# The order of four DMA transposes and two weight loads at the start of a GEGLU kernel

## The chip, the cores and the metric

One core of a Trainium2 chip. The metric is the device time of one execution in microseconds (us). The span, which the profile shows, leaves out what lies around the program: 1.7 to 2.9 us in the runs on record, so the time has a spread of its own that the span has not.

## The reference

```python
B, S, D, F = 1, 2048, 1024, 3584          # everything bf16
def reference(x, w_gate, w_up, w_down):
    return (gelu(x @ w_gate) * (x @ w_up)) @ w_down      # tanh form of GELU
```

## The kernel before

The products are made in halves of S and mostly by a Strassen scheme (the matmuls of L381 and L617). Only the first chunk of 512 columns of F, for the first half of S (1024 tokens), is done with plain products: these are the matmuls of L245, grouped in eight "units". A unit is 128 columns of F by one block of 512 tokens: 8 matmuls of gate and 8 of up, one for each 128-wide block of D. The first two units share their walk through D and are called `first_units`; the third is `unit(hT, PB, 2, 0)`.

x has to be transposed. For the first token block, D blocks 0 to 3 are loaded plainly and transposed by TensorE; D blocks 4 to 7 come by four DMA transposes ("transpose 4" to "transpose 7" below). The first chunk's weights are loaded in two halves of columns: columns 0 to 255 (`FA = 256`), for the first two units, and columns 256 to 511, for the third and fourth, called here the **gate half** (of `w_gate`) and the **up half** (of `w_up`), 512 KB each. SP (SyncE) issues these transfers; the texts below call its queue, or the part of it at one DMA engine, a ring. All that the change touches is the order in which SP issues them, and the order of the 32 matmuls of the first two units:

```python
    for j in range(2):                                   # j: 0 gate, 1 up
        load_w(first, j, KH, KD, sp, 0, FA)              # D blocks 4..7, columns 0..255
    for kd in range(KH, KD):
        load_xT(xT, 0, 0, kd, kd + 1)                    # transposes 4, 5, 6, 7
    for j in range(2):
        load_w(first, j, 0, KD, sp, FA, FG)              # gate half, up half
    for k0 in range(0, KD, KH):
        load_xT(xT, 0, 1, k0, k0 + KH)                   # second token block, 4 D blocks each
    # ... (cut)
    def first_units(hT):
        wg, wu = chunks[first]
        held = (VB, RB)
        transpose_x0(0)
        for q in range(NXQ):                             # pairs of D blocks
            for kd in (2 * q, 2 * q + 1):
                for u in range(2):
                    mm_gu(banks[held[u][0]], wg, u, 0, kd)
            for kd in (2 * q, 2 * q + 1):
                for u in range(2):
                    mm_gu(banks[held[u][1]], wu, u, 0, kd)
                # ... (cut)
```

## Time and profile before

| | before |
|---|---|
| time, median of 6 | 543.49 us (543.32 to 544.40) |
| span of the profiled run | 541.7 us |
| TensorE busy | 533.9 us, 99% |
| first Strassen matmul in the chain that ended last | 34.83 us |
| from there to the start of the last instruction | 503.51 us |

### The profile page before, as it was taken

The page shows a single profiled execution, that of the slowest core. Times are in us where ns is not written, and L with a number is a line of the kernel's source. Part 1 is how long each engine was busy: PE and PEld are TensorE (multiplying, and loading weights), DVE is VectorE, ACT ScalarE, POOL GpSimd, SP SyncE. Part 2 cuts the span into 40 slices and gives each one's busy share as a digit, 9 for nine tenths or more (in the row PEclk, how much of TensorE's full clock was granted, in tenths as well). Part 3 has the DMA queues.
Part 4 walks back from the last instruction along what each step waited for, and adds up shares of the span by engine and source line. Part 5 has one row for each costly group of instructions (what it writes and reads, how often), then busy time and mean ns, then how long its engine had stood idle before and what let it go on. Part 6 is the DMA issues. An engine that isn't in the chain of part 4 may idle for free.

```text
span 541.7 us, 7194 instructions
## 1 busy us (share of the span) xinstructions
PE 533.9 (99%) x2356; PEld 372.6 (69%) x2392; DVE 350.5 (65%) x465; ACT 258.4 (48%) x433; POOL 239.5 (44%) x206
## 2 busy tenths in 40 slices
PE   8999999999999999999999999999999999999997
PEld 3456777777677676767777766777767776866865
DVE  1646666887765899889574444444454469979961
ACT  2345555455555319216455555555555552462270
POOL 0097777888877000000057776677777630000000
PEclk9999999999999999999999999999999999999999
DMA  8956598898836979689952240404040457767946
GB/s 206 299 193 146 166 280 241 171 295 176 265 129 218 347 256 343 215 267 299 324 196 87 70 136 20 156 1 156 0 155 1 157 162 247 252 224 241 290 145 205
DMA packets 85924, 104.80 MB, mean 193 GB/s; under 512 B 18816, under 2 KB 67456, under 8 KB 85888
## 3 DMA queue, kind: packets, MB, share of 16 engines
q1 hardware_dynamic: 84816, 103.83, 61.5%
q10 hardware_dynamic: 1072, 0.52, 0.4%
q8 instruction: 19, 0.31, 0.3%
q14 instruction: 17, 0.14, 0.1%
HBM read 87.03 MB, written 13.63 MB: 186 GB/s over the span
## 4 chain that ended last, share of the span: by engine, by line
PE 96%; DMA 1%; SPq 1%; issue 0%; ACT 0%; ACTq 0%
PE bank L381 60%; PE bank L617 32%; PE bank L245 4%; DMA w_mem<-in_w_gate_dram 1%; SPq L172 1%; ACT o_sb L665 0%; ACTq L665 0%
## 5 line engine op out<-in xcount | busy, mean ns | idle before, releaser
L381 PE MATMUL bank<-t_mem,s_mem 128*128 128x512 f32 x1016 | 249.2, 399 | 0.0
L381 PEld LDWEIGHTS bank<-t_mem,s_mem 128*128 128x128 f32 x1016 | 190.9, 188 | 44.1
L355 POOL TENSOR_TENSOR s_mem<-w_mem 128x512 fp32r<-128x512 bf16 x100 | 117.4, 1194 | 197.7 <-DVE t_mem L238 103.3
L617 PE MATMUL bank<-t_mem,s_mem 128*128 128x512 f32 x560 | 130.2, 392 | 0.0
L404 DVE TENSOR_TENSOR bank<-bank,m 128x512 f32<-128x512 f32 x104 | 72.2, 698 | 83.0 <-ACT bank L424 74.3
L617 PEld LDWEIGHTS bank<-t_mem,s_mem 128*128 128x128 f32 x560 | 105.1, 188 | 22.9 <-issue 0.2
L269 DVE TENSOR_TENSOR hT<-w_mem,bank 128x512 bf16<-128x512 f32 x104 | 71.3, 687 | 59.9 <-ACT w_mem L264 24.8
L264 ACT ACTIVATE w_mem<-bank 128x512 f32<-128x512 f32 x104 | 61.8, 596 | 79.9 <-DVE bank L404 47.3
L381 PE MATMUL bank<-xT,w_mem 128*128 128x512 bf16 x391 | 97.5, 380 | 1.3
L381 PEld LDWEIGHTS <-w_mem 128*128 128x128 bf16 x416 | 36.6, 98 | 50.4 <-issue 13.1
L530 DVE TENSOR_TENSOR t_mem<-w_mem 128x1024 fp32r<-128x1024 bf16 x56 | 65.6, 1218 | 0.0
L355 POOL TENSOR_TENSOR s_mem<-w_mem,s_mem 128x512 fp32r<-128x512 bf16 x50 | 63.3, 1287 | 0.0
L355 POOL TENSOR_TENSOR s_mem<-s_mem,w_mem 128x512 fp32r<-128x512 f32 x50 | 60.3, 1227 | 0.0
L368 ACT CAST s_mem<-w_mem 128x512 fp32r<-128x512 bf16 x52 | 32.0, 616 | 32.6 <-PE bank L381 28.6
L592 DVE TENSOR_TENSOR s_mem<-hT 128x512 fp32r<-128x512 bf16 x56 | 40.5, 755 | 10.5 <-PE bank L617 7.0
L617 PEld LDWEIGHTS <-hT 128*128 128x128 bf16 x224 | 21.3, 98 | 26.6 <-issue 1.8
L419 ACT COPY m<-bank 128x512 f32<-128x512 f32 x52 | 30.6, 588 | 17.1 <-PE bank L381 17.0
L424 ACT COPY bank<-bank 128x512 f32<-128x512 f32 x52 | 29.6, 570 | 17.1 <-PE bank L381 17.1
L415 ACT COPY bank<-bank 128x512 f32<-128x512 f32 x52 | 29.6, 570 | 13.2 <-PE bank L381 13.2
L665 ACT CAST o_sb<-bank 128x512 bf16<-128x512 f32 x28 | 15.4, 585 | 39.7 <-PE bank L617 39.7
L245 PE MATMUL bank<-xT,w_mem 128*128 128x512 bf16 x125 | 28.1, 379 | 1.1 <-DMA w_mem<-in_w_gate_dram 0.7
L527 ACT CAST t_mem<-w_mem 128x1024 fp32r<-128x1024 bf16 x28 | 26.9, 1048 | 0.0
(39 smaller groups left out, 229.2 us busy)
## 6 DMA issues: line engine op xcount, KB each, us to landing
t_mem<-t_dram SPq DMA_DIRECT2D x56, 512.0 KB, 5.1
w_mem<-in_w_gate_dram SPq DMA_DIRECT2D x11, 1024.0 KB, 6.4
w_mem<-in_w_up_dram SPq DMA_DIRECT2D x11, 1024.0 KB, 8.6
wd_sb<-in_w_down_dram SPq DMA_DIRECT2D x28, 256.0 KB, 3.4
t_dram<-o_sb SPq DMA_DIRECT2D x28, 256.0 KB, 2.6
wd_sb<-in_w_down_dram SPq DMA_DIRECT2D x12, 512.0 KB, 8.6
w_mem<-in_w_down_dram SPq DMA_DIRECT2D x10, 512.0 KB, 6.3
w_mem<-in_w_down_dram SPq DMA_DIRECT2D x4, 1024.0 KB, 6.6
```

The source lines that it names most:

```text
L245: nc.tensor.matmul(ps[:], lhsT=w_sb[:, kd, fi * P : (fi + 1) * P], rhs=xT[:, kd, tb * TB : (tb + 1) * TB], start=(kd == 0), stop=(kd == KD ...
L264: act(nc.scalar.activation(out=g_sb, in_=ps[:], func=ACT.Gelu_apprx_tanh))
L269: nc.vector.tensor_tensor(out=hT[:, fc, tb * TB : (tb + 1) * TB], in0=g_sb, in1=ps[:], op=ALU.mult,)
L355: pool(nc.gpsimd.tensor_tensor(out=t, in0=in0, in1=in1, op=op))
L368: act(nc.scalar.copy(out=t, in_=a(1, 1)))
L381: nc.tensor.matmul(banks[bank][:], lhsT=lhs[:, c, :], rhs=rhs[:, c, :], start=start and c == 0, stop=c == KH - 1, skip_group_check=True,)
L404: nc.vector.tensor_tensor(out=banks[dst][:], in0=banks[src][:], in1=m5[j][:], op=ALU.add)
L415: act(nc.scalar.copy(out=banks[QB[j]][:], in_=banks[PB[j]][:]))
L419: act(nc.scalar.copy(out=m5[j][:], in_=banks[VB[j]][:]))
L530: dve(nc.vector.tensor_tensor(out=t, in0=in0, in1=in1, op=ALU.subtract))
L592: dve(nc.vector.tensor_tensor(out=t, in0=in0, in1=in1, op=op))
L617: nc.tensor.matmul(banks[bset[u]][:], lhsT=lhs(i, u), rhs=rhs(i), start=start and i == 0, stop=stop and i == NS - 1, skip_group_check=True,)
```

## The change

Intent: the third unit waited for the gate half, which SP could issue only after four transposes of 1.28 us each. The change issues the gate half between transposes 5 and 6 and the up half after transpose 7. Transposes 6 and 7 then come later, so the first two units take D block by D block, gate and up of a block together, which puts off the first use of block 7.

```diff
-    for kd in range(KH, KD):
-        load_xT(xT, 0, 0, kd, kd + 1)
     for j in range(2):
+        for kd in (KH + 2 * j, KH + 2 * j + 1):
+            load_xT(xT, 0, 0, kd, kd + 1)
         load_w(first, j, 0, KD, sp, FA, FG)
@@ first_units
-        for q in range(NXQ):
-            for kd in (2 * q, 2 * q + 1):
-                for u in range(2):
-                    mm_gu(banks[held[u][0]], wg, u, 0, kd)
-            for kd in (2 * q, 2 * q + 1):
-                for u in range(2):
-                    mm_gu(banks[held[u][1]], wu, u, 0, kd)
-                if kd == 0:
-                    transpose_x0(1)
+        order = [(0, 0), (0, 1), (1, 0), (1, 1)]
+        order += [(j, kd) for kd in range(2, KD) for j in range(2)]
+        for j, kd in order:
+            for u in range(2):
+                mm_gu(banks[held[u][j]], (wg, wu)[j], u, 0, kd)
+            if (j, kd) == (1, 0):
+                transpose_x0(1)
```

## The prediction

> **What bounds the kernel now.** I read the page first: busy shares, slices, the chain that ended last.
>
> ```profile
> PE 533.9 (99%) x2356; PEld 372.6 (69%) x2392; DVE 350.5 (65%) x465; ACT 258.4 (48%) x433; POOL 239.5 (44%) x206
> ...
> PE   8999999999999999999999999999999999999997
> ...
> PEclk9999999999999999999999999999999999999999
> ...
> PE 96%; DMA 1%; SPq 1%; issue 0%; ACT 0%; ACTq 0%
> PE bank L381 60%; PE bank L617 32%; PE bank L245 4%; DMA w_mem<-in_w_gate_dram 1%; SPq L172 1%; ACT o_sb L665 0%; ACTq L665 0%
> ```
>
> TensorE is busy 99% of the 541.7 us span at full clock, and 96% of the chain that ends last is its own matmuls. Only the DMA and SPq shares, about 2%, are not, and the chain in order of time puts all of them in the first 14 us. So I listed what the matmuls wait for, over the whole span:
>
> ```profile
> PE bank L197 <- PEq L898: 0.8, 1, 0.8
> PE bank L245 <- DMA w_mem<-in_w_gate_dram: 0.7, 1, 0.7
> PE bank L295 <- DMA w_mem<-in_x_dram: 0.7, 1, 0.7
> PE bank L245 <- ACT xT L305: 0.2, 1, 0.2
> ```
>
> Four waits, 2.4 us in total. The first is the start of the program, the third the first load of x, the fourth the first transposed block; the change touches none of these. The second is the one it aims at: after the first two units (32 matmuls, L245) TensorE needs columns 256 to 511 of the first chunk of w_gate. The timeline shows when they are asked for:
>
> ```profile
> 4.50 5.12 SPq L172 DMA_TRANSPOSE xT<-in_x_dram  x4
> ...
> 9.66 0.58 SPq L161 DMA_DIRECT2D w_mem<-in_w_gate_dram  x1
> 10.28 0.58 SPq L161 DMA_DIRECT2D w_mem<-in_w_up_dram  x1
> 10.91 6.64 SPq L172 DMA_TRANSPOSE xT<-in_x_dram  x2
> ...
> 13.87 20.96 PE L245 MATMUL bank<-xT,w_mem 128*128 128x512 bf16 x94 [0.72 <-DMA w_mem<-in_w_gate_dram]
> 15.66 18.68 PEld L245 LDWEIGHTS <-w_mem 128*128 128x128 bf16 x88 [0.38 <-DMA w_mem<-in_w_up_dram]
> ```
>
> SP spends 1.28 us on each of four transposes (5.12 / 4) before it issues the gate half at 9.66; that lands at 13.82 and TensorE starts at 13.87. In a narrow timeline the last of the first 32 matmuls starts at 12.77, and 23 intervals before it, at 7.81, the first of D block 2: one per 4.96 / 23 = 0.2157 us. So the next could have started at 12.77 + 0.22 = 12.99. **The gap is 0.88 us** (the wait list says 0.72 because it counts from a matmul's modelled end). The up half costs a little more: eight gate matmuls from 13.87 end at 15.60, and the next starts at 15.66: 0.06. Together 0.94 us, 0.17% of 543.5. No larger gain is in reach of this change.
>
> **What the Trainium skill says.** "TensorE: Matmul & The Clock Gate", Step-by-step, gives about 216 ns between matmuls of 512 columns in a stream; the trace agrees with 215.7. "DMA: Bandwidth & Descriptors", Queues, rings and completion order, says that all DMAs issued by SP share one row of rings and that each DMA engine takes its descriptors in ring order. The trace agrees: the transposes of the second token block were issued from 10.91, but packets under 512 B, which here are transposes, appear only once the two weight halves ahead of them have nearly drained. The two answers are for 13 to 14 and 14 to 15 us:
>
> ```profile
> DMA packets 625, 0.31 MB, mean 315 GB/s; under 512 B 10, under 2 KB 625, under 8 KB 625
> DMA packets 693, 0.28 MB, mean 283 GB/s; under 512 B 264, under 2 KB 693, under 8 KB 693
> ```
>
> The same page, Latency and other measured facts, gives a hardware-generated DMA about 0.6 us to its first byte: the gate half's issue ended at 10.24 and the first packets move at about 10.85, so it agrees. And its Rules for kernel authors say that a transpose beside ordinary DMAs needs no ordering; the built kernel indeed adds no such wait.
>
> **The change, part by part.** It removes and adds no matmul, copy or byte. The built instruction order differs on SP and TensorE only: SP issues transpose 4, transpose 5, gate half, transpose 6, transpose 7, up half (numbers are D blocks); TensorE takes blocks 2 to 7 as gate, up, gate, up rather than in pairs. SP's waits there are for earlier semaphores of DMAs landed by 6.9 us, so none should hold.
>
> SP: gate half issued at 4.50 + 2 x 1.28 = 7.06 instead of 9.66, 2.6 us earlier. Transposes 6 and 7 go 0.62 us later (7.68, 8.96). The up half stays at 10.24 and the second token block's transposes at 10.9.
>
> Gate half: first packets at 7.06 + 1.2 = 8.3. At 10.9 to 11.6 before, it began slowly (about 80 GB/s for 0.75 us) and then ran near 340 GB/s; here the slow part falls under the drain of transposes 4 and 5. My estimate: 0.06 MB by 9.0 and the other 0.46 MB by 10.4, landing at about 11.0. It is needed at 12.99. **That removes the whole 0.88.**
>
> Up half: issued at the same time, but now alone at the front. The gate half took 4.17 us in that position; 10.24 + 4.2 = 14.4, needed at 12.99 + 8 x 0.2157 = 14.72. Removes the 0.06.
>
> Transposes 6 and 7 pay for this. They now sit in the rings behind 512 KB of weights. Before, transpose 6 landed at about 9.95 and 7 at 11.05. After: 6 starts at 10.4, needs 0.5 us for its 128 KB at the 0.26 to 0.29 MB per us seen at 8.4 to 9.4, and some 0.6 from last packet to landing: 11.5. At both places where transposes followed weights (8.0 to 8.4 and 15.2 to 15.4) the rate fell to 80 to 100 GB/s for 0.2 to 0.4 us, so up to 11.8. Transpose 7: 0.4 to 0.5 later, 12.0 to 12.3.
>
> TensorE's new order sets when these are needed. From the narrow timeline, block 2 starts at 7.81 and each block takes 4 x 0.2157 = 0.86, so block 4 is needed at 9.54, 5 at 10.40, 6 at 11.26, 7 at 12.13. (In the old order 7 would be needed at 11.70; that is what the second part buys: 0.43 us for block 7 and for block 5, nothing for block 6.) Block 6 is thus late by 0.2 to 0.55: I take 0.35. Block 7 is then needed at 12.48 and is there. **A new wait of 0.35 us gives back part of the gain.**
>
> Sum: -0.88 - 0.06 + 0.35 = -0.6 us. What follows shifts as a whole: past 14 us TensorE has no wait in the list, and the preparation for the first Strassen pair has slack: s1's last GpSimd sum ends at 28.4 and is used at 36.2. 543.5 - 0.6 = **542.9 us**.
>
> **The rivals.** (a) The gate half really delays the transposes: if the slow start isn't hidden and the switches between copies and transposes cost their dip twice, block 6 lands at about 12.2 and TensorE waits 0.9. The gain is gone: 543.5. For it: the observed dips and the strict ring order. Against: DMA stood idle at 9.4 to 9.75 and 10.6 to 10.85, so there is room. (b) The transposes keep up, because the gate half is through by 10.0: the full 0.94, 542.6. For it: the same idle stretches; against: 512 KB at 340 GB/s is 1.5 us from a start at 8.3 to 9.0. (c) The second token block's later transpose becomes the next bound. It lands at 21.15; its first matmul was due at about 21.7, and would be due at 20.8 after a 0.9 shift: up to 0.4 lost if it stays. Against: SP's first transpose of that block took 4.4 us to issue and the second 2.2, so the first was held back by full queues; with the gate half gone from them both should move earlier. In that case 543.0 to 543.2. (d) Another engine becomes the bound: GELU and the product of the two first units come a few tenths later in the new order, but their banks are used again only 16 matmuls or more on, 3.4 us. I give it nothing.
>
> **Range and chances.** The outcomes lie from 542.5 (b) to 543.6 (a); three runs before spread over 0.23 us, so I add a little on either side. Range 542.3 to 543.7. A change of 2% would be 10.9 us; the only waits touched sum to 0.94, so faster by over 2% has 0.01, slower 0.01 (it would need a stall ten times anything seen here), within 2% 0.98.
>
> **What would show it.** In the changed kernel: the gate half issued near 7.1; no wait of L245 for w_gate; a wait for xT instead, 0.2 to 0.5 us, near 11.3; the first matmul of the third unit at 13.2 to 13.5 instead of 13.87; no wait for w_up near 15; and everything from there earlier by that difference, first matmul of L381 at about 34.1 for 34.67. Wrong would be: a wait for xT of 0.9 or more (a), none at all (b), a wait for xT near 21 (c), or a time below 542.3, which would mean gaps that I don't see.

## The result

543.88 us (543.11 to 544.32, 6 runs) against 543.49 us: ratio 1.0003, with a 95% interval of 0.9990 to 1.0016. Ratios here are from the runs of both kernels in the same rounds, so not quite the ratio of the medians. By its time alone, the change can't be told from no change at all.

The profile tells more. The wait list of TensorE in the changed kernel (what waited, for what: us in total, times, longest):

```profile
PE bank L197 <- PEq L896: 0.8, 1, 0.8
PE bank L245 <- DMA xT<-in_x_dram: 0.5, 1, 0.5
```

The wait for `w_gate` has gone and a wait for `xT`, a transposed block, has come. The timeline of SP and TensorE (start, duration, what, and in brackets the idle time before it and what ended it) shows the new order:

```profile
4.17 2.51 SPq L172 DMA_TRANSPOSE xT<-in_x_dram  x2
...
6.72 0.58 SPq L161 DMA_DIRECT2D w_mem<-in_w_gate_dram  x1
...
7.34 2.73 SPq L172 DMA_TRANSPOSE xT<-in_x_dram  x2
...
10.12 0.58 SPq L161 DMA_DIRECT2D w_mem<-in_w_up_dram  x1
10.74 5.91 SPq L172 DMA_TRANSPOSE xT<-in_x_dram  x2
11.84 22.61 PE L245 MATMUL bank<-xT,w_mem 128*128 128x512 bf16 x101 [0.55 <-DMA xT<-in_x_dram]
```

The gate half was issued 2.55 us after the first transpose began instead of 5.16 (9.66 - 4.50), as intended, and landed at 11.15. But TensorE's first matmul of block 6 started at 11.84, when transpose 6 landed. The matmul before it started at 10.91 and the spacing is 0.2157, so the gap is 11.84 - 10.91 - 0.22 = 0.71 us. The gap removed was 0.88.

Where the transfers stood is seen from the packets of the stretch from 9 to 10 us, first before, then after. Packets under 512 B are the transposes':

```profile
DMA packets 523, 0.13 MB, mean 126 GB/s; under 512 B 523, under 2 KB 523, under 8 KB 523
```

```profile
DMA packets 600, 0.31 MB, mean 307 GB/s; under 512 B 0, under 2 KB 600, under 8 KB 600
```

Before, this microsecond moved transposes and nothing else, at less than half the mean rate, since the DMA engines stood nearly idle from 9.4 to 9.7. After, it moved weights and not one packet of a transpose, although transpose 6 had been issued at 7.34. In the next microsecond, 10 to 11, the transposes return (under 512 B 565).

Finally the chain of the two kernels, at the first Strassen matmuls (start, duration, what), before and after:

```profile
34.83 12.82 PE bank L381 x57
```

```profile
34.45 12.82 PE bank L379 x57
```

This pair of traces shows 0.38 us gained. But in the changed kernel's run the very first load of x landed 0.34 us sooner (first transpose of TensorE at 4.42 instead of 4.76), and D block 2 was started at 7.68 instead of 7.81. Nothing in the change is as early as that, so these 0.13 us of the 0.38 belong to the run. More traces of the same kernels were therefore part of the experiments.

### The profile page after: what moved, and what is told of

It reads as the page before. It is cut to its first block, busy times and chain, and to the rows that moved or that the text cites. A ratio compares the mean times of both kernels' runs of the same rounds, so it can differ in the third digit from the quotient of the medians.

```text
span 541.3 us, 7194 instructions
## 1 busy us (share of the span) xinstructions
PE 534.5 (99%) x2356; PEld 373.1 (69%) x2392; DVE 350.6 (65%) x465; ACT 258.4 (48%) x433; POOL 239.7 (44%) x206
## 4 chain that ended last, share of the span: by engine, by line
PE 97%; DMA 1%; SPq 1%; issue 0%; ACT 0%; ACTq 0%
PE bank L379 60%; PE bank L615 32%; PE bank L245 4%; DMA xT<-in_x_dram 1%; DMA w_mem<-in_w_gate_dram 1%; SPq L172 0%; ACT o_sb L663 0%; SPq L161 0%; ACTq L663 0%
## 5 line engine op out<-in xcount | busy, mean ns | idle before, releaser
L417 ACT COPY m<-bank 128x512 f32<-128x512 f32 x52 | 30.6, 589 | 17.1 <-PE bank L379 17.0
L245 PE MATMUL bank<-xT,w_mem 128*128 128x512 bf16 x125 | 28.0, 379 | 0.8 <-DMA xT<-in_x_dram 0.5
```

The source lines that it names most:

```text
L245: nc.tensor.matmul(ps[:], lhsT=w_sb[:, kd, fi * P : (fi + 1) * P], rhs=xT[:, kd, tb * TB : (tb + 1) * TB], start=(kd == 0), stop=(kd == KD ...
L417: act(nc.scalar.copy(out=m5[j][:], in_=banks[VB[j]][:]))
```

## The experiments

One theory and two rivals. **Ring order:** the weights are put into the rings ahead of transposes 6 and 7, which therefore land later by the time those bytes take; the new wait is the price of the removed one. Rival: a fixed cost of putting any copy between transposes. Rival: the new matmul order itself costs or saves the time. What the expectations call the stretch starts at the first matmul of D block 2. It ends at the third unit's first matmul in order_only, dma_only, double_dose and gate_after_6, and at the first matmul of that unit's up product in the others.

The table has all traces. "6 after 5" is the landing of transpose 6 less that of transpose 5 (landing is issue plus the time to landing that the DMA view gives, which is rounded, so this column is good to about 0.1 us); a gap is the time between the starts of two matmuls less the usual spacing of 0.2157, good to 0.01 or 0.02 us; "Strassen" is the start of the first Strassen matmul in the chain, "rest" from there to the start of the last instruction.

| kernel (one trace each) | KB ahead of 6 | 6 after 5 | gap for a transpose | gap for gate half | gap for up half | Strassen | rest | span |
|---|---|---|---|---|---|---|---|---|
| before | 0 | 0.49 | 0 | 0.88 | 0.05 | 34.83 | 503.5 | 541.7 |
| before_again | 0 | 0.53 | 0 | 0.89 | 0.01 | 34.58 | 503.6 | 541.5 |
| order_only | 0 | 0.49 | 0 | 0.83 | 0.05 | 34.96 | 504.3 | 542.6 |
| half_dose | 256 | 1.51 | 0 | 0 | 0.52 | 34.38 | 503.5 | 541.3 |
| half_dose_timed | 256 | 1.52 | 0 | 0 | 1.24 | 34.74 | 503.5 | 541.6 |
| changed | 512 | 2.61 | 0.71 | 0 | 0 | 34.45 | 503.5 | 541.3 |
| after_again | 512 | 2.41 | 0.58 | 0 | 0.20 | 34.52 | 503.5 | 541.3 |
| dma_only | 512 | 3.02 | 0.68 + 0.09 | 0 | 0 | 35.03 | 503.7 | 542.0 |
| fill_gap | 512 | 2.52 | 0 | 0 | 0.26 | 34.24 | 503.5 | 541.0 |
| fill_gap_again | 512 | 2.39 | 0 | 0 | 0.30 | 34.35 | 503.9 | 541.5 |
| double_dose | 1024 | 4.57 | 2.59 | 0 | 0 | 36.58 | 503.5 | 543.4 |
| gate_after_6 | 0 | 0.48 | 0.66 (block 7) | 0 | 0.23 | 35.22 | 503.5 | 542.0 |
| fill_up_on_act | 512 | 2.72 | 2.41 (block 7) | 0.32 | 0 | 36.32 | 504.4 | 544.0 |

### order_only: the new matmul order without the new DMA order

```diff
 # against the changed kernel: the DMAs as before
-    for j in range(2):
-        for kd in (KH + 2 * j, KH + 2 * j + 1):
-            load_xT(xT, 0, 0, kd, kd + 1)
-        load_w(first, j, 0, KD, sp, FA, FG)
+    for kd in range(KH, KD):
+        load_xT(xT, 0, 0, kd, kd + 1)
+    for j in range(2):
+        load_w(first, j, 0, KD, sp, FA, FG)
```

> Only the new matmul order; the DMAs as before. Measure: start of the third unit minus start of D block 2, 5.18 us if 24 matmuls run without a gap; 6.06 in the kernel before, 5.90 in the changed one. Ring-order theory (the 512 KB of weights in front of transposes 6 and 7 delay them): no wait for xT, the old wait for the gate half, 6.06 again. Rival, the matmul order itself costs time: gaps among blocks 2 to 7 although every transposed block has landed, more than 6.06.

Measured: 13.99 - 7.98 = 6.01 us, the old gap, no wait for `xT`, and the matmuls of blocks 2 to 7 at their spacing. The matmul order by itself neither costs nor saves. The single time, 545.21 us against 543.43, is not evidence on this: Strassen starts 0.13 us later than in the first trace of before; 0.8 us more was lost after 186 us, where the wait list has 0.2 us for a reload of `t_mem` from DRAM that the edit doesn't touch. This loss goes with the run and not with the kernel: of the two traces of the filled gap below, which are of one kernel, fill_gap has none (rest 503.5) and fill_gap_again lost 0.4 us at 272 us, where such a reload had just landed (rest 503.9). Why a run has it is open, but it can be as large as all that the change could gain.

### dma_only: the new DMA order without the new matmul order

```diff
 # against the kernel before: only the first hunk of the change
-    for kd in range(KH, KD):
-        load_xT(xT, 0, 0, kd, kd + 1)
     for j in range(2):
+        for kd in (KH + 2 * j, KH + 2 * j + 1):
+            load_xT(xT, 0, 0, kd, kd + 1)
         load_w(first, j, 0, KD, sp, FA, FG)
```

> Only the new DMA order; matmuls in the old order. Ring-order theory: block 6 is needed at the same matmul in both orders, so the same wait of about 0.72 us for it, and block 7, needed 0.43 us later, is there: 5.90, as the changed kernel. Rival, the second part of the change is what limits the damage: block 7 is also waited for, 6.1 or more.

Measured: stretch to the third unit 14.15 - 8.21 = 5.94 us; a gap of 0.68 for block 6 and one of 0.09 for block 7. So the second part of the change is worth at most 0.09 us here: both orders need block 6 at the same matmul, and that is the block that is late. 543.82 us in one run against 543.43.

### half_dose and double_dose: how the delay depends on the bytes ahead

```diff
 # half_dose, against the changed kernel
-    for j in range(2):
-        for kd in (KH + 2 * j, KH + 2 * j + 1):
-            load_xT(xT, 0, 0, kd, kd + 1)
-        load_w(first, j, 0, KD, sp, FA, FG)
+    for kd in (KH, KH + 1):
+        load_xT(xT, 0, 0, kd, kd + 1)
+    load_w(first, 0, 0, KH, sp, FA, FG)              # 256 KB of the gate half
+    for kd in (KH + 2, KH + 3):
+        load_xT(xT, 0, 0, kd, kd + 1)
+    load_w(first, 0, KH, KD, sp, FA, FG)             # the other 256 KB
+    load_w(first, 1, 0, KD, sp, FA, FG)
```

```diff
 # double_dose, against the changed kernel
+    for kd in (KH, KH + 1):
+        load_xT(xT, 0, 0, kd, kd + 1)
     for j in range(2):
-        for kd in (KH + 2 * j, KH + 2 * j + 1):
-            load_xT(xT, 0, 0, kd, kd + 1)
         load_w(first, j, 0, KD, sp, FA, FG)
+    for kd in (KH + 2, KH + 3):
+        load_xT(xT, 0, 0, kd, kd + 1)
```

> 256 KB of the gate half (its first four D blocks) between transposes 5 and 6, the rest after transpose 7, then the up half. In the changed kernel block 6 started 4.17 us after block 2. Ring-order theory: 256 KB less in front of transpose 6, 0.75 us at 340 GB/s, so it starts at about 3.45, where it is due, and the wait is 0 to 0.1. Rival, a fixed cost of putting any copy between transposes, whatever its size: still about 4.17. The up half is issued 0.6 us later than in the changed kernel: a new wait for it of 0.2 to 0.6.

> Gate half and up half, 1 MB, both between transposes 5 and 6. Ring-order theory: 512 KB more in front of transpose 6, about 1.5 us more: block 6 starts 5.7 us after block 2 instead of 4.17, a wait of about 2.2, third unit at about 7.4. Rival, a fixed switch cost: only SP's 0.6 us of issue is added at most, block 6 at 4.2 to 4.8.

Measured: 0, 256, 512 and 1024 KB ahead put transpose 6 some 0.5, 1.5, 2.5 (2.4 to 3.0) and 4.6 us behind transpose 5. That is a line: about 1.0 us for each 256 KB. A fixed cost would have given one step; it falls. (All these weights move in packets of 512 B, so bytes and number of packets grow together, and the runs don't tell them apart.) The chains show the same, with transpose 6 from issue to landing in the changed kernel and in the double dose:

```profile
7.34 4.45 DMA xT<-in_x_dram
```

```profile
8.27 5.66 DMA xT<-in_x_dram
```

The half dose has no wait for a transpose left, but the up half, issued behind one more load, is now late. The double dose made the predicted wait, a little longer (2.59 instead of 2.2). From their wait lists, half dose first (its line numbers are three higher than in the changed kernel, those of the double dose two):

```profile
PE bank L197 <- PEq L899: 0.8, 1, 0.8
PE bank L298 <- DMA w_mem<-in_x_dram: 0.6, 1, 0.6
PE bank L248 <- DMA w_mem<-in_w_up_dram: 0.4, 1, 0.4
...
```

```profile
PE bank L247 <- DMA xT<-in_x_dram: 2.4, 1, 2.4
...
```

The list counts from a matmul's modelled end, some 0.16 us after the next could have started; hence 2.4 for the 2.59 of the table. Single times: 543.05 and 545.25 us against 543.43.

### after_again: the changed kernel once more

No edit.

> The changed kernel again, unedited, for the spread. Measured by the start of the third unit's up product minus the start of D block 2 (6.90 us without a gap; 7.85 in the trace before, 7.61 in the changed one, so 0.24 apart). Theory: transpose 6 lands 2.6 us after transpose 5 again, within 0.4, and the stretch is 7.6 +- 0.2; the time is within 0.1% of before, since runs of one kernel spread by 1 us. Rival, the 2.6 was an accident of one run: transpose 6 lands under 2.2 us after 5 and the stretch is 7.3 or less.

Measured: transpose 6 landed 2.41 us after transpose 5, and the stretch was 15.35 - 7.66 = 7.69. The delay is no accident. 543.48 us (543.16 to 545.28, 6 runs), ratio 1.0009 (0.9997 to 1.0021). Here, too, the up half was late, by 0.20, so the gaps add to 0.78 against 0.93 before.

### half_dose_timed

The half dose again, with five rounds.

> The half dose again, timed. Its trace had no wait for a transpose and a wait of 0.52 us for the up half; stretch of third unit's up product 7.43 against 7.85 before. Expected: 7.4 to 7.5 again, time 0.3 to 0.5 us under before, ratio 0.9991 to 0.9995, so not clear of noise if the spread is as before. Rival, the gain in the stretch is lost later: the first Strassen pair starts no earlier relative to block 2 than in the kernel before (26.86 us).

Measured: a miss. This time the gap for the up half was 1.24 us instead of 0.52; the stretch was 15.58 - 7.43 = 8.15. Part of it is that TensorE began block 2 at 7.43, 0.35 us sooner than in the first trace, and simply waited longer; the up half itself landed at 15.53 instead of 15.16. 543.67 us, ratio 1.0004 (0.9992 to 1.0016): no gain.

### fill_gap: other work in the place of the wait

```diff
 # against the changed kernel
         for j, kd in order:
+            if (j, kd) == (0, 6):
+                for k in range(KH):
+                    mm_gu(banks[PB[0]], wg, 2, 0, k)     # third unit, gate, blocks 0..3
             for u in range(2):
 # and in unit(): the third unit's gate product goes on from block 4
```

> The changed kernel with one edit: four gate matmuls of the third unit (D blocks 0 to 3, their weights landed) are taken before block 6, where TensorE waited 0.72 us. Theory that the wait for block 6 is the whole loss: the wait is gone, block 6 due 0.86 us later than its landing allows; the up half, landed 7.04 us after block 2 in the changed kernel, becomes the next wait, 0.1 to 0.2: stretch 7.0 to 7.15, 0.7 to 0.85 below before, time 542.7 if before is 543.45 (ratio 0.9985). Rival, the gate half itself is not there when the four are taken, or the transposes land later still: stretch 7.4 or more.

Measured: stretch 15.07 - 7.90 = 7.17; no wait for a transpose, and the up half late by 0.26, a little over what was expected. The wait list shows nothing but the program's start:

```profile
PE bank L197 <- PEq L900: 0.8, 1, 0.8
```

(The gap of 0.26 is less than a matmul's modelled tail plus the list's smallest entry and so isn't in it; it was read from matmul starts.) The Strassen matmuls start at

```profile
34.24 15.96 PE bank L383 x71
```

which is 0.59 before the first trace of before and 0.34 before the second. 543.09 us against 543.44, ratio 0.9997 (0.9985 to 1.0009): less than the 0.9985 that was expected, and not clear of noise. The four matmuls need the gate half sooner, and little was to spare: it landed at 11.15, and they were due at about 11.35.

### gate_after_6: the weights one transpose later

```diff
 # against the changed kernel (its loop over j is replaced)
+    for kd in (KH, KH + 1, KH + 2):
+        load_xT(xT, 0, 0, kd, kd + 1)
+    load_w(first, 0, 0, KD, sp, FA, FG)
+    load_xT(xT, 0, 0, KH + 3, KH + 4)
+    load_w(first, 1, 0, KD, sp, FA, FG)
```

> Gate half between transposes 6 and 7 instead of 5 and 6. Ring-order theory: transpose 6 lands about 0.5 us after 5 as before, and the 2.0 us per 512 KB falls on transpose 7: it lands 2.5 us after 6, about 4.7 after block 2, where 4.32 is due: a wait of 0.3 to 0.5 for block 7 and none for 6; third unit at 5.5 to 5.7. Rival, transposes are delayed by the copy wherever it stands (shared bandwidth and no order): block 6 is waited for too.

Measured: transpose 6 landed 0.48 after transpose 5 and was not waited for; transpose 7 landed 3.33 us after 6 (0.80 to 1.20 with nothing between them), and block 7 was late by 0.66. Only what stands behind the weights is delayed. The delay was above the expected 2.5, and the wait above the 0.3 to 0.5; the up half, too, was late, by 0.23. One run, 543.78 us.

### before_again: a second trace of the kernel before

No edit.

> The kernel before, unedited, for a second trace. Theory now: in both kernels TensorE's place after the third unit is set by the transfers, so it follows the issue of the first transpose, not TensorE's own start. From that issue to the first Strassen matmul: 30.3 us in the trace before, 30.3 and 30.3 in the two of the changed kernel. Expected 30.3 +- 0.2 here too. Rival, the changed kernel gains 0.3 us and start luck hides it: 30.6 or more here.

Measured: first transpose issued at 4.07, Strassen at 34.58, so 30.51. It lies at the edge: just outside the 0.2 that I allowed and short of the rival's 30.6. Two traces of each kernel are too few to say that TensorE's place follows that issue alone. What they do say is the size: 34.83 and 34.58 before, 34.45 and 34.52 after, on average 0.22 us apart, which is what the gaps give (0.93 and 0.90 against 0.71 and 0.78, 0.17 on average).

### fill_gap_again

The filled gap once more, with five rounds.

> The filled gap again, timed, to see whether its span is really shorter: it was 541.0 in the trace, median 541.1 of five, against 541.6 of eleven before. Theory: no wait for a transpose, one for the up half of 0.1 to 0.4; median span 541.0 to 541.3; ratio 0.998 to 0.9995. Rival, chance: the span is 541.5 or more, the time that of before.

Measured: no wait for a transpose again, 0.30 for the up half. The median span was 541.15 us against 541.6 of before in the same rounds, as it was 541.1 against 541.6 the first time. 543.00 us (542.77 to 543.84) against 543.48, ratio 0.9989 (0.9976 to 1.0002). Each interval still holds 1; both medians and both median spans are lower by 0.35 to 0.5 us, a little less than the 0.6 to 0.7 us by which the gaps fell (0.93 and 0.90 to 0.26 and 0.30). So a gain is likely, but not shown by the times.

### fill_up_on_act: the up half from another queue

```diff
 # against fill_gap: SP no longer issues the up half; the scalar engine does, behind its second copy
             if (j, kd) == (1, 0):
                 transpose_x0(1)
+                load_w(first, 1, 0, KD, act, FA, FG)
```

> The filled gap, with the up half issued from the scalar engine's queue behind its second copy instead of SP's behind transpose 7. It waits for transpose 4 to land (8.8 to 9.0), so it is issued at about 9.0 instead of 10.0 and isn't behind transpose 7 in the ring. Theory that the queue order delays the up half: it lands at about 14.0 rather than 15.0, due at 14.8, no wait, 0.2 to 0.3 us faster than the filled gap. Rival, bytes are the limit: in its own ring it takes turns with transposes 6 and 7 and the second token block's, which then land later, and it lands at 14.7 or later, or blocks 6 or 7 are waited for: no faster than the filled gap.

Measured: the rival, and worse than it. The up half, issued at 8.73, landed at 15.34; transpose 7, issued at 8.78, needed 6.6 us to land instead of the 3.2 to 3.5 in the filled gap and landed at 15.40. TensorE waited for it, and before that 0.32 us for the gate half, which the four matmuls needed sooner than in the filled gap, as TensorE was earlier:

```profile
PE bank L246 <- DMA xT<-in_x_dram: 2.2, 1, 2.2
...
PE bank L621 <- DMA t_mem<-t_dram: 0.6, 1, 0.6
```

546.01 us against 543.48, ratio 1.0044 (1.0029 to 1.0060), the one experiment that is clear of noise. The second line is the late reload of `t_mem` that order_only and fill_gap_again also had. 0.9 us of this trace's time was lost there (rest 504.4), so not all of the 0.44% is shown to come from the edit.

How the two queues shared the DMA engines can be read from the packets by queue. From 11.0 to 12.5 us, with transpose 6 through and transpose 7 issued long before, they moved (q10 carries the up half, q1 all that SP issues):

```profile
q10 hardware_dynamic: 667, 0.34, 86.3%
q1 hardware_dynamic: 57, 0.01, 4.0%
```

In the filled gap, half a microsecond from 11.0 on was enough for a whole transpose:

```profile
DMA packets 531, 0.13 MB, mean 259 GB/s; under 512 B 525, under 2 KB 531, under 8 KB 531
```

So the two queues did not take even turns here: for 1.5 us the copy moved almost alone and transpose 7 hardly at all, although the copy was in the other queue. Why is open.

## Why the prediction was right

**The bound.** Right. At most 0.94 us could be had, and nothing past 34.8 us moved: the rest is 503.5 us before and after.

**Minus 0.88 for the gate half.** Right. It was issued at 6.72 (predicted 7.06; that run began 0.33 earlier), landed at 11.15 (predicted 11.0), and no trace of the changed kernel waits for it. From its issue it took 4.4 us and not the predicted 3.9, which did no harm here, but is part of the error in the term for transpose 6.

**Minus 0.06 for the up half.** Not reliable. It was on time in one trace of the changed kernel and late by 0.20 in the other, so that the term is anything from -0.05 to +0.15. I had given it the 4.17 us that the gate half took before; it took 4.6 and 5.2.

**Plus 0.35 for transpose 6.** The mechanism was right, the size was not, and this is the step that failed in the sum: 0.71 and 0.58 us. I counted the 512 KB at 340 GB/s with the slow start hidden under the drain of transposes 4 and 5, and put transpose 6 at 11.5 to 11.8, 2.0 to 2.3 us behind transpose 5 at 9.46. Measured were 2.4 to 2.6 (3.0 in one related run). The doses give the figure to use: 1.0 us for each 256 KB, so about 260 GB/s in this mix, not 340. Part of it can be seen: from 8 to 9 us, with transposes and weights together, the rate was 230 GB/s, and from 9 to 10 us, with weights alone, 307.

**Block 7 is there.** Right: no gap before it in either trace. And the second part of the change, as the prediction says, does nothing for block 6; it was worth 0.09 us in dma_only.

**The sum.** -0.6 predicted; by the gaps -0.22 and -0.12 (0.71 and 0.78 against the first trace's 0.93 and the second's 0.90), -0.22 by the Strassen starts. The truth lies between the predicted way and rival (a), which had the gain gone through a wait of 0.9. Rival (b), transposes that keep up, fell. Rival (c), the second token block, did not come: its second transpose landed at 20.5 (20.9 in the second trace), sooner than before (21.1), as argued, and nothing waited for it. Rival (d), another engine, did not come either: no such wait is new in the lists.

**The time.** 542.9 predicted in 542.3 to 543.7, ratio near 0.9989; measured ratio 1.0003 and 1.0009 in the two sets of rounds. Within 2% was right, but that was the safe part: all the outcomes that were considered lie within 0.2% of before. The measured median, 543.88, lies a little above the range's end; this was the part taken too narrowly, as spans of the same kernel ran from 541.2 to 542.2 in one set of rounds and to 543.5 in the next. The half of the twelve spans of the changed kernel that are 541.2 to 541.4 lie below the median of before, 541.6; the other half are 541.9 and more, and why its runs fall into two groups was not settled. The late reload of `t_mem`, which cost 0.4 to 0.9 us in three of the thirteen traces, would be enough for it; no slow span of the changed kernel was traced, so this is not shown. The two median spans of the changed kernel are 541.6 and 541.65, that of before in the second set of rounds is 541.6: by the spans, too, nothing was gained that can be seen.

## What to carry to other kernels

A transfer moved up in a queue is paid for by those that it overtakes. Before moving it, list which consumers stand behind the overtaken ones and when they are due, and price the bytes at the rate that the mix of copies and transposes really reaches, not at the best rate of copies (here 260 against 340 GB/s). When the queue can't deliver everything in time, reorder the consumer instead: four matmuls whose data had landed, put where the wait was, took away the wait for the transpose (an up half late by 0.26 to 0.30 us remained), while splitting the load, moving it by one place, or using a second queue only moved the wait elsewhere.

## What the Trainium skill lacked or had wrong

- "DMA: Bandwidth & Descriptors", Queues, rings and completion order: its ring order was borne out; it lacks what standing behind a copy costs a DMA transpose. The runs show 1.0 us for each 256 KB of weights ahead (0.5, 1.5, 2.5 and 4.6 us for 0, 256, 512 and 1024 KB).
- The same page, Rules for kernel authors: "A transpose next to ordinary DMAs needs nothing". That held for the results, which were correct in every run, but the rule says nothing of the time, and no page gives what a transpose loses to a copy on the other queue: with the up half on the scalar engine's queue, transpose 7 took 6.6 us to land instead of 3.2 to 3.5, and from 11.0 to 12.5 us the copy moved 667 packets against 57 of SP's queue.
- "TensorE: Matmul & The Clock Gate", What's actually happening, is agreement and not a lack: it says that the moment at which TensorE goes from slow to full rate varies by 500 ns either way, and that one kernel had 6 to 14 slow matmuls. The trace agrees that it varies: the first six matmuls of L245 took 1.46 us in the kernel before and 1.93 us in dma_only, with nothing waited for between them. So the same start can differ by 0.5 us, more than the change was worth.
